# An attention and expert-layer kernel: 36 operations of a computed schedule go back to where the scheduler puts them

## Chip, cores, metric

The kernel runs on one core of a Trainium2 chip. Its time is the device time of one execution in microseconds (us); the profile is the hardware profiler's record of one execution. TensorE (PE) multiplies matrices, VectorE (DVE), ScalarE (ACT) and GpSimd (POOL) do the elementwise work, SyncE (SP) and ScalarE issue the transfers (DMA).

## The reference

Attention over 4 batches, 8 heads, 768 positions and 64 features, in which each query sees its neighbours (less than 16 positions away) and one summary key and value for each block of 32 positions; its output, 3072 tokens of 512 features, goes through a layer with a softmax gate and a layernorm:

```python
k_sum = k.reshape(B, H, nb, block, D).max(axis=3)
v_sum = v.reshape(B, H, nb, block, D).mean(axis=3)
scores_l_m = np.where(mask_l, scale * q @ k.T, -1e9)          # |i - j| < 16
scores_s = scale * einsum('bhsd,bhnd->bhsn', q, k_sum) + log(block)
a = softmax(concat([scores_l_m, scores_s]))
x = (a @ concat([v, v_sum])) as (3072, 512)
h = x @ w_in                                                  # (512, 1024)
solu = h * softmax(h)
ln = (solu - mean) / sqrt(var + 1e-6) * g_ln
return ln @ w_out                                             # (1024, 512)
```

(The lines are shortened to what is computed.)

## The kernel before

The 3072 tokens are worked on in 24 tiles of 128. Every float32 product with weights is made of three: a value is split into a part rounded to the matmul's format (names ending in h: xh, lh, and the first half of w) and the rest (xl, ll), and TensorE adds low·high, high·low and high·high in PSUM, about 0.23 us each. For the first eight tiles `first` (line 949) multiplies each tile with w_in into the banks h; from then on `first_two` (968) takes two tiles at once with seven block products in place of eight, into hu, hf and hl, for which ws_own, ws_v, w1s, w3s (sums of blocks of weights) and sums (sums of blocks of x) are made once on VectorE, GpSimd and ScalarE. `second` (1144) multiplies with w_out into the bank o, from which ScalarE (1150) or VectorE (1152) writes os; a transfer takes os to the output from ScalarE's queue (1154).

The attention of a step goes: scores into the PSUM tiles s_0l, s_0r (695); VectorE adds the mask, gives e and the negative maximum nm (714); ScalarE's exponentials (722) with their sum z; VectorE's 1/z (728); e times 1/z on VectorE or GpSimd (406, 407); transposes on TensorE into t_0l, t_0r (750), copied to at (399, 400); products with the values into x (797); x is split into xh (399) and xl (406, 806). The layer between is: hm, the row maximum of h, and its sign turned (1026, 1028); ScalarE's exponentials he (1031); hz, its inverse (1034, 1037); VectorE's he times h (1039) with the mean nmu (1042); ScalarE's centring (1051) and sq, the sum of squares (1054); GpSimd's tiny operations for y (1057 to 1064); transposes or a pass through memory (lt, tbl) and the split into lh and ll. Weights raw are converted through cv to w by integer operations (490 to 525). kw are keys with their block maxima ksum (562), vt values, to which the transfer of line 658 adds the block means vsum.

The PSUM tiles that end in l and r are two halves of one buffer, each in a bank of its own (`halves=True`); this stays.

The program has no loop on the chip: Python writes out every instruction. Each operation is recorded by `op` in an object of class `Plan`, with a cost for each engine that could do it, and given to the engines by `issue`. `issue` works out a due time for each operation, changes due times by a list of fixed random seeds (`SEARCHED`), and `order` then simulates a list schedule: it gives each operation an engine, a start and a place. In the kernel before, `move` comes after it: for each of 36 entries (number of the operation, engine, number of another operation) it takes the operation out of its line and puts it behind the other in the line of the engine named, using that engine's form of it, and merges the lines again. Each engine runs its own line in order, and waits for the others by semaphores. The zero matmuls of line 1336 are put in by `issue` where TensorE would have waited by the plan, in the first 80 us of it.

Of the kernel before, what the change touches and what calls it, by code (L numbers as in the profile page):

```python
# [63 lines left out]
class Buf:  # L64


    def __init__(self, make, prev=()):
        self.make, self.prev, self.tile = make, prev, None
        self.ops, self.writers, self.readers, self.gone = [], {}, {}, False
# [16 lines left out]
class Plan:  # L86
# [29 lines left out]

    MOVES = ((77, "act", 109), (290, "act", 294), (242, "act", 290), (214, "act", 301), (391, "act", 354),
        (540, "act", 547), (602, "act", 582), (613, "act", 612), (664, "act", 668), (679, "act", 672),
        (1396, "act", 1196), (1875, "act", 1855), (100, "dve", 45), (146, "dve", 130), (203, "dve", 155),
        (322, "dve", 388), (314, "dve", 364), (371, "dve", 314), (452, "dve", 410), (419, "dve", 418),  # L120
        (663, "dve", 560), (706, "dve", 707), (678, "dve", 660), (869, "dve", 812), (1223, "dve", 1222),
        (1287, "dve", 1224), (1864, "dve", 1874), (606, "pool", 1150), (561, "pool", 606), (615, "pool", 585),
        (562, "pool", 615), (589, "pool", 588), (680, "pool", 1154), (814, "pool", 1300), (753, "pool", 1302),
        (909, "pool", 1303),)

    def __init__(self):
        self.ops, self.rings, self.banks, self.idle, self.slots = [], {}, {}, None, []
        self.turns, self.homes, self.last, self.shrunk = {}, {}, {}, set()
# [75 lines left out]
    def issue(self):  # L204

        for o in self.ops:
            o.left = len(o.deps)
            for d in o.deps:
                d.users.append(o)
        sorted_ = [o for o in self.ops if not o.left]  # L210
        for o in sorted_:
            for u in o.users:
                u.left -= 1
                if not u.left:
                    sorted_.append(u)
        for o in reversed(sorted_):
            o.due = min([u.due for u in o.users] + ([o.prio] if "pe" in o.can else []), default=o.prio)
            if "sp" in o.can:
                o.due = o.prio
        for seed in self.SEARCHED:  # L220
            self.shift(seed)
        order = self.move(self.order())
        at, done = self.START, set()
        for o in order:
            if o.engine == "pe":
                while at + self.SYNC < min(o.start + o.late, self.FILL):
                    at += self.keep_up(at, done)
                at = max(at - o.late, o.start) + o.cost * (2 if o.start < self.COLD else 1)
            done.add(o)
            o.fn()  # L230

    def move(self, order):


        moved = {self.ops[o]: (e, self.ops[p]) for o, e, p in self.MOVES}
        key = {o: float(i) for i, o in enumerate(order)}
        lines = {}
        for o in order:
            if o not in moved:
                lines.setdefault(o.engine, []).append(o)  # L240
        todo = list(moved)
        while todo:
            o = next(x for x in todo if moved[x][1] not in todo)
            todo.remove(o)
            e, p = moved[o]
            lines[e].insert(lines[e].index(p) + 1, o)
            key[o] = key[p] + 0.01
            o.engine, (o.cost, o.fn) = e, o.can[e]
            o.start = min(o.start, p.start)
        done, out = set(), []  # L250
        while any(lines.values()):
            heads = [x[0] for x in lines.values() if x and x[0].deps <= done]
            o = min(heads, key=key.get)
            lines[o.engine].pop(0)
            done.add(o)
            out.append(o)
        return out

    def shift(self, seed):

# [1121 lines left out]
```

## Time and profile before

| | |
|---|---|
| median of 3 runs | 360.62 us (360.47 to 361.37) |
| the profiled execution | 360.37 us, of which the span of its instructions 358.6 us |
| granted TensorE clock | 1.00 over the whole span |
| TensorE busy | 353.7 us, 99% of the span |
| VectorE, ScalarE, GpSimd busy | 300.5, 279.9, 159.4 us (84, 78, 44%) |
| the chain that ended last | 88% TensorE, 4% ScalarE, 4% transfers, 2% VectorE |

The span is from the first instruction to the last; the time has 1.77 us more around it. A busy TensorE is at work on some matmul; a hole is time in which it waits. The rows further down give for each instruction its start, its duration and, in brackets, how long its engine stood idle ahead of it and for what.

### The profile page before, as it was taken

To read this page: it belongs to the slowest core of one execution; us is meant where nothing else is said; L and a number is where in the kernel's file an instruction comes from. 1 tells how busy PE (TensorE), PEld (TensorE's weight loads), DVE (VectorE), ACT (ScalarE), POOL (GpSimd) and SP (SyncE) were. 2 spreads that over 40 slices of the span, in tenths; PEclk is the share of its full clock that TensorE was granted. 3 is DMA by queue.
4 is the path that set the end of the run, shared out by engine and by line. 5 is a ranking of instruction groups with operands and counts; after the bars stand their busy time and mean duration, and the time that the engine had idled before them with its cause. 6 is when DMAs were issued, how large, how long until landed. Compare 5 with 4: busy or idle time off the path is not lost.

```text
span 358.6 us, 9381 instructions
## 1 busy us (share of the span) xinstructions
PE 353.7 (99%) x3332; PEld 277.3 (77%) x3332; DVE 300.5 (84%) x962; ACT 279.9 (78%) x814; POOL 159.4 (44%) x293
## 2 busy tenths in 40 slices
PE   8999999999999999999999999999999999999996
PEld 3538767778777887787888888888888888888886
DVE  4989999998999998998699998887897996947331
ACT  4888998998869988799698696895896896946320
POOL 6612430267869899225815247150335054533300
PEclk9999999999999999999999999999999999999999
DMA  7999994144525445448389393475264282344711
GB/s 248 417 412 406 357 409 162 62 115 148 172 69 185 137 149 193 141 158 289 101 275 290 112 277 131 128 255 172 80 208 148 59 287 90 117 149 153 229 58 58
DMA packets 28530, 68.19 MB, mean 190 GB/s; under 512 B 3852, under 2 KB 13324, under 8 KB 26948
## 3 DMA queue, kind: packets, MB, share of 16 engines
q1 hardware_dynamic: 24620, 60.87, 50.6%
q10 hardware_dynamic: 3864, 6.74, 5.3%
q8 instruction: 26, 0.43, 0.5%
q14 instruction: 20, 0.16, 0.1%
HBM read 49.55 MB, written 15.73 MB: 182 GB/s over the span
## 4 chain that ended last, share of the span: by engine, by line
PE 88%; ACT 4%; DMA 4%; DVE 2%; issue 0%; POOL 0%; ACTq 0%
PE o L1144 36%; PE hu L968 13%; PE h L949 10%; PE x L797 6%; PE hl L968 6%; PE hf L968 3%; DMA qt<-in_q 2%; PE s_0l L695 2%; PE s_1l L695 2%; PE t_0l L750 2%; PE t_1l L750 2%; ACT e L722 2%; PE vs_ps L582 1%; PE vs_ps L1336 1%; DMA raw<-in_w_in 1%; PE x L1336 1%
## 5 line engine op out<-in xcount | busy, mean ns | idle before, releaser
L1144 PE MATMUL o<-w,lh 128*128 128x512 f32 (+1 forms) x400 | 128.1, 386 | 0.0
L1144 PEld LDWEIGHTS o<-w,lh 128*128 128x128 f32 x400 | 74.1, 188 | 15.6 <-issue 0.6
L1144 PE MATMUL o<-w,ll 128*128 128x512 f32 (+1 forms) x200 | 76.2, 381 | 0.0
L722 ACT ACTIVATE e<-e,nm 128x120 f32<-128x120 f32 x192 | 73.3, 389 | 0.0
L949 PE MATMUL h<-w,xh 128*128 128x512 f32 x128 | 43.0, 400 | 0.2 <-DVE he L1039 0.2
L1144 PEld LDWEIGHTS o<-w,ll 128*128 128x128 f32 x200 | 37.6, 188 | 6.8
L722 ACT ACTIVATION_READ_ACCUMULATOR e<-e,nm 128x1 f32 x192 | 37.3, 194 | 0.0
L949 PEld LDWEIGHTS h<-w,xh 128*128 128x128 f32 x128 | 24.0, 188 | 7.0 <-ACT at L399 0.8
L1051 ACT ACTIVATE he<-he,nmu 128x512 f32<-128x512 f32 x36 | 24.9, 722 | 4.0 <-DVE nmu L1042 3.6
L407 POOL TENSOR_TENSOR ll<-lt,lh 128x512 fp32r<-128x512 f32 x11 | 16.0, 1466 | 26.1 <-DVE lh L400 19.2
L797 PEld LDWEIGHTS x<-at,vt 120*64 120x64 f32 (+1 forms) x768 | 24.4, 138 | 4.1 <-issue 2.4
L624 POOL TENSOR_TENSOR st_v<-st_v 96x512 f32<-96x512 f32 (+3 forms) x28 | 23.0, 830 | 8.3 <-DMA st_v<-in_vb 7.7
L797 PE MATMUL x<-at,vt 120*64 120x64 f32 (+1 forms) x768 | 26.5, 224 | 0.0
L1074 DVE STREAM_TRANSPOSE tbl<-he 128x1024 f32<-128x1024 f32 x18 | 22.3, 1239 | 4.4 <-ACT he L1051 2.3
L1054 ACT ACTIVATE sq<-he 128x1024 bf16<-128x1024 f32 x24 | 25.4, 1057 | 0.1
L949 PE MATMUL h<-w,xl 128*128 128x512 f32 x64 | 25.1, 393 | 0.0
L1031 ACT ACTIVATE he<-hs,hm 128x512 f32<-128x512 f32 x24 | 17.2, 719 | 9.1 <-DVE hm L1021 9.1
L406 DVE TENSOR_TENSOR e<-e,z 128x960 f32<-128x960 f32 x18 | 22.3, 1238 | 0.1
L1150 ACT ACTIVATE os<-o,y 128x512 f32<-128x512 f32 x19 | 13.1, 687 | 11.7 <-PE o L1144 11.5
L407 POOL TENSOR_TENSOR xl<-sums,xh 128x256 fp32r<-128x256 f32 (+1 forms) x12 | 12.4, 1035 | 19.4 <-ACT xh L399 19.4
L401 POOL COPY kw<-ksum 128x192 f32<-128x192 f32 x21 | 8.5, 406 | 26.8 <-PE s_0r L695 20.7
L406 DVE TENSOR_TENSOR ll<-lt,lh 128x512 fp32r<-128x512 f32 x25 | 19.6, 802 | 0.5 <-ACT lh L399 0.3
(250 smaller groups left out, 972.1 us busy)
## 6 DMA issues: line engine op xcount, KB each, us to landing
vt<-in_v SPq DMA_DIRECT2D x12, 1024.0 KB
farl<-tbl SPq DMA_DIRECT2D x18, 512.0 KB
lt<-farl SPq DMA_DIRECT2D x72, 128.0 KB
kraw<-in_k SPq DMA_DIRECT2D x16, 400.0 KB
out<-os ACTq DMA_DIRECT2D x23, 256.0 KB
qt<-in_q SPq DMA_DIRECT2D x11, 512.0 KB
raw<-in_w_in SPq DMA_DIRECT2D x8, 512.0 KB
raw<-in_w_out SPq DMA_DIRECT2D x8, 512.0 KB
```

The source lines that it names most:

```text
L406: by = {dve: lambda: nc.vector.tensor_tensor(out=to(), in0=a(), in1=b(), op=kind), pool: lambda: nc.gpsimd.tensor_tensor(out=to(), in0=a() ...
L407: pool: lambda: nc.gpsimd.tensor_tensor(out=to(), in0=a(), in1=b(), op=kind)}
L624: op(pool, 0.15 + w * 0.0021, lambda w=w, o=o: nc.gpsimd.tensor_tensor(out=o.ap[:n, :w], in0=x.ap[:n, :w], in1=x.ap[:n, w:2 * w], op=ALU.add),
L722: nc.scalar.activation(out=e.ap[:, n, :], in_=e.ap[:, n, :], func=AF.Exp, bias=nm.ap[:, n:n + 1], scale=-1.0, accum_out=z.ap[:, n:n + 1])
L797: nc.tensor.matmul(xp()[j * D:(j + 1) * D, i, qs], vs.ap[:k, u, cs], at.ap[:k, u % 2, n[j] + u // 2, :], start=not apart, stop=not apart o ...
L949: nc.tensor.matmul(hp.ap, a.ap[:, c, ts], w.ap[:, i], start=(c == 0 and n == 0), stop=(c == NKC - 1 and n == 2))
L968: nc.tensor.matmul(to.ap, operand(y, n)[:, c], w(c).ap(i), start=first and c == 0 and k == 0, stop=c == 1 and k == 2, skip_group_check=True)
L1031: op(act, 0.71, lambda i=i, hp=hp: nc.scalar.activation(out=part(i), in_=hp(), func=AF.Exp, bias=nm.ap, accum_out=zs.ap[:, i:i + 1]), r=[k ...
L1051: (act, 0.57, lambda sl=sl: nc.scalar.activation(out=e.ap[:, sl], in_=e.ap[:, sl], func=AF.Identity, bias=nmu.ap))], port=True)
L1054: op(act, 1.13, lambda: nc.scalar.activation(out=sq.ap, in_=e.ap, func=AF.Square, accum_out=ss.ap), r=[e], w=[sq, ss])
L1074: op(dve, 1.13, lambda: nc.vector.transpose(out=tb.ap.rearrange("p (q c a) -> p q c a", q=4, a=32), in_=of().rearrange("p (c q a) -> p q c ...
L1144: nc.tensor.matmul(o.ap[:, cols], a.ap[:, f, :], w.ap[:, i, cols], start=(f == 0 and n == 0), stop=(f == NFC - 1 and n == 2))
```

## The change

The table `MOVES` and the function `move` go, and `issue` takes the schedule as `order` gives it:

```diff
-    MOVES = ((77, "act", 109), (290, "act", 294), (242, "act", 290), (214, "act", 301), (391, "act", 354),
...
-        order = self.move(self.order())
+        order = self.order()
...
-    def move(self, order):
-
-
-        moved = {self.ops[o]: (e, self.ops[p]) for o, e, p in self.MOVES}
...
```

TensorE's and SyncE's lines stay the same, instruction for instruction. Thirty of the 36 operations change only their place on their engine. Six change the engine: one high part of a weight conversion (cv_494) from VectorE to ScalarE, the last half of the last output (os) from VectorE to ScalarE, a cast of xh (128x256) from ScalarE to VectorE, and a subtraction xl (128x256) and two additions ws_own (128x512) from GpSimd to VectorE. The line numbers of the kernel after are lower by 36 for all that stands below `move`.

At three places the rows of the program show what changes. The first is ScalarE at about 31 us, where the second half of a tile's xh is cast and the transfer of the block means into vt is issued. Before:

```order
L399 CAST w_578<-cv_494 128x512
L501 ACTIVATE cv_549<-raw_109 128x512
L399 CAST xh_0_119<-x_0_1_554 128x512
L658 DMA vt_1_111<-vsum_114 24x4x512
L399 COPY kw_2_0_609<-kraw_0_155 128x8x96
```

And after:

```order
L363 CAST w_578<-cv_521 128x512
L465 ACTIVATE cv_549<-raw_109 128x512
L622 DMA vt_1_111<-vsum_114 24x4x512
L363 CAST xh_0_119<-x_0_1_554 128x512
L363 COPY kw_2_0_609<-kraw_0_155 128x8x96
```

The cast of xh, which VectorE's xl waits for, has gone behind the issue of the transfer.

The second is at 128 to 138 us: GpSimd, whose line held the subtraction xl and the two additions ws_own around the multiplication of e (e_2_0) by z. Before:

```order
L624 TENSOR_TENSOR st_v_0_0_1744<-st_v_0_0_1744 96x256
L407 TENSOR_TENSOR xl_1_2015<-sums_1_2020,xh_1_2007 128x256
L407 TENSOR_TENSOR ws_own<-w_578,ws_own 128x512
L1058 TENSOR_SCALAR ss_2086<-ss_2086 128x1
L407 TENSOR_TENSOR e_2_0_2022<-e_2_0_2022,z_2_0_2052 128x960
L407 TENSOR_TENSOR ws_own<-ws_own,w_578 128x512
L1060 TENSOR_TENSOR y_202<-ss_2086,mhalf 128x1
```

And after, where these three are gone from it:

```order
L588 TENSOR_TENSOR st_v_0_0_1744<-st_v_0_0_1744 96x256
L1022 TENSOR_SCALAR ss_2086<-ss_2086 128x1
L1024 TENSOR_TENSOR y_202<-ss_2086,mhalf 128x1
L371 TENSOR_TENSOR e_2_0_2022<-e_2_0_2022,z_2_0_2052 128x960
L1021 TENSOR_TENSOR ss_2086<-ss_2086,y_202 128x1 x2
```

VectorE has them in the same stretch after the change, between the maxima hm, the tiny hm of line 1028 (992 after), the block maxima ksum and 1/z:

```order
L364 CAST ws_v<-ws_own 128x512
L370 TENSOR_TENSOR xl_1_2015<-sums_1_2020,xh_1_2002 128x256
L370 TENSOR_TENSOR ws_v<-ws_own,ws_v 128x512
L526 TENSOR_REDUCE ksum_1_2088<-kraw_1_1932 128x24
L990 TENSOR_REDUCE hm_2098<-h_0_2057 128x1
L990 TENSOR_REDUCE hm_2098<-h_1_2035 128x1
L692 RECIPROCAL z_2_0_2052<-z_2_0_2052 128x8
L370 TENSOR_TENSOR ws_own<-w_578,ws_own 128x512
L992 TENSOR_TENSOR hm_2114<-hm_2098 128x1
L526 TENSOR_REDUCE ksum_1_2088<-kraw_1_1932 128x24
L370 TENSOR_TENSOR ws_own<-ws_own,w_578 128x512
L998 TENSOR_SCALAR hz_2121<-hz_2121 128x1
```

Three two-input operations came over, and the tiny hm, for which ScalarE's exponentials wait, has one of them ahead of it.

The third is the end of ScalarE's line, where the last two halves of the output leave. Before (both halves were made by VectorE):

```order
L1150 ACTIVATE os_5147<-o_5093,y_4963 128x512
L1154 DMA out<-os_5147 128x512
L1154 DMA out<-os_5180 128x256
L1154 DMA out<-os_5183 128x256
L1378 UNCONDITIONAL_BRANCH
```

And after:

```order
L1114 ACTIVATE os_5147<-o_5093,y_4963 128x512
L1118 DMA out<-os_5147 128x512
L1114 ACTIVATE os_5180<-o_5127,y_5010 128x256
L1118 DMA out<-os_5180 128x256
L1118 DMA out<-os_5183 128x256
L1342 UNCONDITIONAL_BRANCH
```

The half that TensorE finishes last (o_5127) is now made by ScalarE itself, and both issues stand behind it.

## Rows read from the trace of the kernel before

**Rows 1.** The page: busy us, share of the span and instructions of each engine.

```profile
PE 353.7 (99%) x3332; PEld 277.3 (77%) x3332; DVE 300.5 (84%) x962; ACT 279.9 (78%) x814; POOL 159.4 (44%) x293
```

**Rows 2.** Two stretches: start:end and length, busy us (instructions) of each engine, clock, DMA.

```profile
50.00:75.00 25.00, 24.52 (x257) 18.67 (x253) 24.31 (x82) 22.14 (x66) 6.57 (x10) 1.00 0.43 154
110.00:137.00 27.00, 27.00 (x290) 22.04 (x283) 26.12 (x78) 24.17 (x81) 24.30 (x29) 1.00 0.42 144
```

**Rows 3.** The page: the chain that ended last, by engine.

```profile
PE 88%; ACT 4%; DMA 4%; DVE 2%; issue 0%; POOL 0%; ACTq 0%
```

**Rows 4.** Timeline of ScalarE and its queue at 31 us: start, duration, instruction.

```profile
31.19 1.43 ACTq L658 DMA_DIRECT2D vt<-vsum  x1
31.27 0.56 ACT L399 CAST xh<-x 128x512 fp32r<-128x512 f32 x1
```

**Rows 5.** Timeline of VectorE at 33 us.

```profile
32.94 0.68 DVE L806 TENSOR_TENSOR xl<-x,xh 128x512 fp32r<-128x512 f32 x1
```

**Rows 6.** Timeline of TensorE at 33.7 us.

```profile
33.67 0.51 PE L949 MATMUL h<-w,xl 128*128 128x512 f32 x1
```

**Rows 7.** Timeline of VectorE at 42 to 44 us.

```profile
42.21 0.75 DVE L1039 SCALAR_TENSOR_TENSOR he<-h,hz,he 128x512 f32<-128x512 f32 x1
...
44.04 0.68 DVE L1026 TENSOR_REDUCE hm<-h 128x1 f32<-128x512 f32 x1
```

**Rows 8.** Timeline of TensorE at 43.4 us.

```profile
43.43 0.58 PE L949 MATMUL h<-w,xh 128*128 128x512 f32 x1
```

**Rows 9.** Timeline of ScalarE and its queue, 54 to 57 us.

```profile
54.96 0.59 ACT L399 CAST lh<-lt0l 128x512 fp32r<-128x512 f32 x1 [1.34 <-PE lt0r L750]
55.02 0.81 ACTq L658 DMA_DIRECT2D vt<-vsum  x1
55.88 0.72 ACT L523 ACTIVATE w<-cv,g_sb 128x512 fp32r<-128x512 f32 x1 [0.33 <-DVE nm L714]
```

**Rows 10.** Timeline of VectorE at 57 us.

```profile
57.10 0.69 DVE L1122 TENSOR_TENSOR ll<-lt0r,lh 128x512 fp32r<-128x512 f32 x1 [0.44 <-ACT lh L399]
```

**Rows 11.** Timeline of TensorE at 67 us.

```profile
66.95 0.50 PE L949 MATMUL h<-w,xh 128*128 128x512 f32 x1 [0.24 <-DVE he L1039]
```

**Rows 12.** Timeline of ScalarE, 117 to 123 us.

```profile
117.21 0.59 ACT L399 COPY at<-t_0r 120x512 f32<-120x512 f32 x1 [0.21 <-PE t_0r L750]
...
122.27 0.62 ACT L399 COPY at<-t_1l 120x512 f32<-120x512 f32 x1
```

**Rows 13.** Timeline of TensorE at 123 us.

```profile
122.99 0.28 PE L695 MATMUL s_0l<-kw,qt 64*64 64x120 f32 x1
```

**Rows 14.** Timeline of VectorE, 131 to 139 us.

```profile
131.83 1.01 DVE L1028 TENSOR_TENSOR hm<-hm 128x1 f32<-128x1 f32 x1
...
138.08 0.76 DVE L853 TENSOR_TENSOR sums<-x,sums 128x256 f32<-128x256 f32 x2 [1.48 <-ACT xh L399]
138.75 0.68 DVE L406 TENSOR_TENSOR xl<-x,xh 128x512 fp32r<-128x512 f32 x1
```

**Rows 15.** All instructions of line 1028: duration in ns, least/median/most, first and last start.

```profile
L1028 DVE TENSOR_TENSOR hm<-hm x8: 107/169/1012, 39.4 to 131.8; 128x1 f32<-128x1 f32 x8
```

**Rows 16.** Timeline of GpSimd, 130 to 135 us.

```profile
130.83 0.74 POOL L407 TENSOR_TENSOR xl<-sums,xh 128x256 fp32r<-128x256 f32 x1
131.53 1.29 POOL L407 TENSOR_TENSOR ws_own<-w,ws_own 128x512 f32<-128x512 f32 x1
...
133.18 1.79 POOL L407 TENSOR_TENSOR e<-e,z 128x960 f32<-128x960 f32 x1
```

**Rows 17.** Timeline of TensorE at 140 us.

```profile
139.98 0.39 PE L968 MATMUL hf<-w,xl 128*128 128x512 f32 x1
```

**Rows 18.** Timeline of VectorE and of ScalarE's queue at the end, 352 to 358.6 us.

```profile
353.37 0.48 DVE L1152 TENSOR_SCALAR os<-o,y 128x256 f32<-128x256 f32 x1 [7.27 <-PE o L1144]
...
353.88 2.34 ACTq L1154 DMA_DIRECT2D out<-os  x2
...
355.37 0.48 DVE L1152 TENSOR_SCALAR os<-o,y 128x256 f32<-128x256 f32 x1 [1.52 <-PE o L1144]
```

More of the change, by code (lines that the diff above doesn't have):

```diff
@@ L115 @@
         -704973400, 25379729, -590422927, -115574272, -202041329, -486402956,
-    MOVES = ((77, "act", 109), (290, "act", 294), (242, "act", 290), (214, "act", 301), (391, "act", 354),
[L118 to L124, printed above, removed]
     def __init__(self):
@@ L230, in issue @@
             o.fn()
-    def move(self, order):
-        moved = {self.ops[o]: (e, self.ops[p]) for o, e, p in self.MOVES}
[L236 to L257, printed above, removed]
     def shift(self, seed):
```

## The prediction

> **What bounds the kernel now.** I read the page first. TensorE is busy in all but five of 358.6 us [rows 1], and the chain that ended last is 88% TensorE [rows 3]: TensorE is the clock, so a change that leaves its instructions and their order alone can only put holes between them or close holes. The order of the two programs on TensorE and SyncE is the same instruction for instruction, the zero matmuls included. So the prediction is a list of holes. The table by stretches says where there is room for any [rows 2]: in 50 to 75 us TensorE is 24.52 of 25 busy and VectorE 24.31, the one stretch where VectorE and ScalarE feed TensorE just in time (the chain runs there over the two of them); in 110 to 137 us TensorE is full, but VectorE has 26.12 of 27 us of work, ScalarE 24.17 and GpSimd 24.30, so little slack is left for anything late. From 75 us on TensorE runs back to back, and what it loses there it keeps to the end. Only behind its last matmul does another engine end the run.
>
> Thirty of the moved operations stay on their engine and only change place; six also change engine. For each I took from the trace when it ended, who used its result first and how long that user could have waited. Most come out at nothing: their result is used half a microsecond or more after the new end too, and the matmuls that stand in TensorE's queue ahead of the user are the cover. Five places are left.
>
> **Place 1, 31 us: +0.34.** Before, ScalarE rounds xh (31.27) ahead of the issue of the vt transfer, which then occupies its queue from 31.19 to 32.62 [rows 4]: the issue was reached early and waited beside the cast. After, the issue stands first (see the order of ScalarE), and the cast comes behind it, 32.66 to 33.24 in place of 31.84 by the 0.56 of its row plus sequencing. VectorE's xl, which needs it and started 32.94 [rows 5], then starts about 33.28, 0.34 later, and the xl matmul at 33.67 [rows 6] had been waiting for exactly that xl (32.94 + 0.68 = 33.62), so TensorE gets the whole 0.34. Bounds: nothing, if the issue takes less time there (the same line took 0.81 at 55.02 [rows 9], which would end it at 32.0, early enough); 0.34, if it takes its 1.43 again. I take 0.34, since it is the same issue after the same landing.
>
> **Place 2, 44 us: +0.25.** VectorE's hm (0.68, of which about 0.60 shows as step to the next instruction) goes from behind two he operations to ahead of them. The first he ended at 42.96 (42.21 + 0.75) [rows 7], and frees the PSUM bank for the matmul at 43.43 [rows 8], which stands behind six zero matmuls in TensorE's queue: 0.47 of slack less what a semaphore takes. An end at 43.6 makes it start at about 43.68: +0.25, and 0 if the zero matmuls run late too.
>
> **Place 3, 50 to 75 us: −0.44, a gain.** Before, ScalarE holds the lh cast and a DMA issue ahead of w (55.88): it idles 1.34 us for the transposes and another 0.33 [rows 9]. After, w goes first, into that idle time, and the second lh cast can follow the first at about 55.5 (54.96 + 0.59) and not only behind w at 56.5 (55.88 + 0.72, less the overlap): up to 1.0 earlier. VectorE waits for this second lh 0.44 us [rows 10], its one idle time for ScalarE there. A queue that is otherwise full gains what it idled: 0.44, and the matmul at 66.95, which waits 0.24 for VectorE's he [rows 11], and those at 75 us come earlier. Bounds: −1.0, the whole of ScalarE's gain, and 0, if ScalarE gives it back (a 0.84 us copy of kw goes from 73.89 to about 60.5).
>
> **Place 4, 117 to 143 us: +0.77.** Two things add up. (a) The at copy that ran at 117.21, ahead of two exponentials that waited for VectorE's hm, goes behind them [rows 12]: ScalarE loses an idle half microsecond that it had used, and all behind it is 0.5 later. The at copy at 122.27 ended 122.89, and the scores matmul, which takes over its PSUM banks, started 122.99 [rows 13]: 0.10 of slack, so +0.40. (b) Three tensor_tensor operations, 0.74 and twice about 1.29 on GpSimd [rows 16], return to VectorE: two of 0.69 (as VectorE's 128x512 in [rows 10]) and one of half the columns, 0.42 with its fixed part (an estimate from those), 1.80 together. VectorE idles 1.48 us at 138.08 for ScalarE's xh [rows 14], so this alone would be nearly hidden, and it saves something: its tiny hm [128,1] took 1.01 us at 131.83 where the median of eight is 0.17 [rows 14, 15], and it ended at 132.84, GpSimd's ws_own (131.53 + 1.29) at 132.82 [rows 16]. So a two-input operation of VectorE waited for one of GpSimd to its end. That 0.84 goes with ws_own. But then hm stands directly behind ws_own on VectorE, and GpSimd's e multiply (1.79, [rows 16]) is ready as soon as z is done, one place ahead of ws_own: it waits for VectorE's port, gets it next, and hm, or the second ws_own, waits 1.79. The balance on VectorE is 1.80 − 0.84 + 1.79 − 1.48 = 1.27 late at xl, which ended 139.43 (138.75 + 0.68); the hf matmul that reads it ran at 139.98 [rows 17], 0.55 later, of which a semaphore takes some 0.05. So TensorE gets 1.27 − 0.50 = 0.77, and (a)'s 0.40 lies inside it. Bounds: 0 (an earlier hole moves TensorE so that both fit) and 0.40 + 1.79 = 2.19 (the wait falls where nothing is idle). The cast of xh that comes over from ScalarE at 123 us (0.29 on VectorE) is in the noise of these.
>
> The Trainium skill, SBUF — State Buffer, section Who interferes with whom, says that a VectorE instruction with two SBUF inputs contends with a GpSimd instruction that reads SBUF, and that whoever issues second is blocked until the first has finished; issue order decides. By that rule the e multiply blocks hm only if it issues first, else it waits itself: the term would be +0.77 by the first and +0.40 by the second. The row at 131.83 agrees that the loser waits to the end of the other; no row shows who is served first when both wait.
>
> **Place 5, the end: +0.34.** Before, both halves of the last output are written by VectorE, at 353.37 and 355.37, and each is sent off at once; the second issue ends at 356.22 (353.88 + 2.34), and the span 2.38 us later [rows 18]. After, the last half is made by ScalarE, and both issues stand behind it on ScalarE's queue, so the half that was ready at 353.85 leaves last. The os on ScalarE starts when VectorE's did and takes about as long (estimate from [rows 18]: 0.48), so the first issue ends at 356.22, and a second of 0.34 follows: the span ends 0.34 later. Upper bound 0.68 (both transfers also share the way). Nothing lies beside it.
>
> **Sum.** 0.34 + 0.25 − 0.44 + 0.77 + 0.34 = 1.26 us on the profiled execution's 360.37 (a span of 358.6 and 1.77 around it): 361.63. The median of the runs, 360.62, lies 0.25 above the profiled one; with that, 361.9. The bounds: lowest 0 + 0 − 1.0 + 0 + 0.34 = −0.66, 360.0; highest 0.34 + 0.25 + 0 + 2.19 + 0.68 = 3.46, 364.1, and 0.5 more for the seven moves behind 162 us, which I cost at nothing.
>
> **Rivals.** *The port isn't lost* (chance 0.25): VectorE's instructions follow each other without a gap and hm keeps ahead of the e multiply. Then place 4 costs 0.40, the sum is 0.34 + 0.25 − 0.44 + 0.40 + 0.34 = 0.89, the time 361.5. For it: VectorE needs no semaphore from another engine there. Against: hm's 1.01 us [rows 14] is the same meeting, and there VectorE lost. *All hidden but the end* (0.10): zero matmuls and slack take up places 1, 2 and 4, and 3 gains nothing; 0.34 stays: 361.0. The change would in effect do nothing. *Faster* (0.13): place 3 gives the whole 1.0 and TensorE has it at 75 us, while places 1, 2 and 4 are hidden: −0.66, 360.0; below 359.5 it decides only if the stretch 50 to 75 us gains more than 1.4 us, that is, if w, brought forward, also lets the he and xl chain behind it close up. Rows 2 speak against that: VectorE has only 25 − 24.31 = 0.69 us of idle time there, so this is the ceiling for anything that VectorE passes on. *More than the sum* (0.10): the port wait of 1.79 falls where nothing covers it, or one of the moves after 162 us costs too: 363.3 to 364.6.
>
> **How the numbers follow.** Forecast 361.9, with 0.42 for it (361.4 to 362.7). Range 360.2 to 364.2. A measurement of this kernel tells 0.3% from no change, 1.1 us: faster is below 359.5, slower above 361.7. Slower: the larger part of the forecast's case (0.33), the worst one (0.10) and a part of the rival at 361.5 (0.09), 0.52. Faster: the better half of its rival, 0.07. The rest, 0.41, is the same.
>
> **What would show it.** Right: the cast of xh ends after 33.2 and the first xl matmul behind it slips; w runs in the idle time before lt0r's cast and VectorE's 0.44 at 57 us is gone; the scores matmul of 122.99 starts later against the matmuls before it; a VectorE operation of 1 to 2 us of the shape [128,1] or ws_own at 133 to 135 us; the two last issues back to back. Wrong: TensorE shows new idle time elsewhere, above all after 150 us, or as much idle time as before and a span that differs only at the end.

## The result, and the profile after

| | before | after |
|---|---|---|
| median | 360.72 us (6 runs, 360.47 to 361.37) | 362.95 us (6 runs, 362.47 to 363.39) |
| ratio to before | | 1.0060, 95% interval 1.0047 to 1.0072 |
| the profiled execution, and its span | 360.37 us, 358.64 us | 363.39 us, 361.67 us |

The kernel after is slower by 2.23 us, 0.6%. The forecast was 361.9 with a range of 360.2 to 364.2: the direction and the range held, the size was 1.0 us short. Why it was short, and which terms were right only by luck, is the rest of this document.

The page of after answers to [rows 1] and [rows 3]: busy times, and the chain that ended last.

```profile
PE 353.7 (98%) x3332; PEld 277.0 (77%) x3332; DVE 305.6 (84%) x964; ACT 281.2 (78%) x815; POOL 158.7 (44%) x290
...
PE 78%; DVE 12%; ACT 3%; DMA 3%; SPq 1%; issue 1%; ACTq 0%; DVEq 0%
```

TensorE does the same 353.7 us of work in a longer span, so holes were added and no work; VectorE's part of the chain went from 2% to 12%. TensorE's waits (line waited for: us in total, times, longest) name most of them:

```profile
PE vs_ps L1300 <- DVE zero L388: 1.0, 1, 1.0
PE o L1108 <- DVE w L489: 0.9, 1, 0.9
PE s_1l L659 <- DMA qt<-in_q: 0.9, 1, 0.9
PE s_0l L659 <- DMA qt<-in_q: 0.5, 1, 0.5
PE s_1l L659 <- ACT at L363: 0.4, 1, 0.4
PE s_0l L659 <- issue: 0.3, 1, 0.3
```

The first is there before too. The list holds only waits of some length; the 0.24 us at 34 us in the next table is not in it. Since TensorE's instructions are the same and in the same order, the start of one matmul in both timelines says how late TensorE is there, and a place's cost is the step between two such points:

| matmul (line of before) | before | after | late by | step |
|---|---|---|---|---|
| vs_ps (582) | 19.95 | 20.54 | 0.58 | 0.58, loads at the start |
| h (949) | 34.24 | 35.05 | 0.82 | 0.24, place 1 |
| h (949) | 45.48 | 46.52 | 1.03 | 0.21, place 2 |
| h (949) | 66.95 | 67.64 | 0.69 | −0.34, place 3 |
| s_0l (695), behind o | 76.42 | 77.90 | 1.48 | 0.79, place 3, not foreseen |
| s_0l (695) | 122.99 | 124.76 | 1.78 | 0.30, place 4a |
| s_1l (695) | 137.27 | 139.63 | 2.36 | 0.58 |
| s_1r (695) | 137.28 | 140.12 | 2.84 | 0.48 |
| hl, second (968) | 143.43 | 145.99 | 2.56 | −0.28; place 4b with the two above 0.78 |
| end of the execution | 360.37 | 363.39 | 3.02 | 0.46, place 5 |

From 146 us to the last matmul TensorE stays 2.56 to 2.57 late. So this execution is 3.02 us longer, of which 0.58 arises before any moved operation: TensorE waits for the first loads of the queries there. The second profile of after, below, shows that this part is chance, and not the change. (The 0.54 for the end in two of the expectations below was taken from spans rounded to tenths; it is 0.46.)

VectorE's timeline of after at 74 us (start, duration, instruction) and GpSimd's show the step of 0.79, with the matmul of TensorE that waits for it:

```profile
73.99 0.63 DVE L770 TENSOR_TENSOR xl<-x,xh 128x512 fp32r<-128x512 f32 x1
74.55 1.94 DVE L489 SCALAR_TENSOR_TENSOR w<-cv,g_sb,w 128x512 fp32r<-128x512 f32 x1
```

```profile
74.15 1.79 POOL L371 TENSOR_TENSOR e<-e,z 128x960 f32<-128x960 f32 x1
```

```profile
76.54 0.50 PE L1108 MATMUL o<-w,lh 128*128 128x512 f32 x1 [0.89 <-DVE w L489]
```

The weights w take 1.94 us where the eight of this line have a median of 0.75 (only one other is long, 1.23 at 72.73, behind GpSimd's cv). GpSimd's e multiply runs until 75.94, and w ends 0.55 after that. The matmul o that needs this w starts at 76.54. At 135 us it is the same meeting, and the one that the prediction named; VectorE's and GpSimd's timelines of after:

```profile
134.52 0.18 DVE L692 RECIPROCAL z<-z 128x8 f32<-128x8 f32 x1
134.63 0.63 DVE L370 TENSOR_TENSOR ws_own<-w,ws_own 128x512 f32<-128x512 f32 x1
135.19 1.74 DVE L992 TENSOR_TENSOR hm<-hm 128x1 f32<-128x1 f32 x1
```

```profile
134.78 2.13 POOL L371 TENSOR_TENSOR e<-e,z 128x960 f32<-128x960 f32 x1 [0.70 <-DVE z L692]
```

e begins at 134.78, is held up by ws_own (its 1.79 becomes 2.13), and then keeps hm, 128 numbers, until 136.91; hm ends at 136.93. (The texts below call this the port, or the lock: one of the two engines waits until the other's whole operation is done.) The meeting of before, 1.01 us, is in [rows 14 to 16]. ScalarE idles 3.69 us ahead of the exponentials, which wait for hm, and its two at copies come behind them; TensorE's scores wait for these copies:

```profile
136.96 0.69 ACT L995 ACTIVATE he<-h,hm 128x512 f32<-128x512 f32 x1 [3.69 <-DVE hm L992]
...
139.00 0.58 ACT L363 COPY at<-t_0l 120x512 f32<-120x512 f32 x1
139.48 0.59 ACT L363 COPY at<-t_0r 120x512 f32<-120x512 f32 x1
```

```profile
139.63 0.41 PE L659 MATMUL s_1l<-kw,qt 64*64 64x120 f32 x2 [0.40 <-ACT at L363]
140.12 0.31 PE L659 MATMUL s_1r<-kw,qt 64*64 64x120 f32 x1
```

s_1l starts when the first copy has ended (139.58), s_1r when the second has (140.07): these are the steps of 0.58 and 0.48.

At 32 us ScalarE's xh stands behind the issue, as the order says (ScalarE and its queue, answering to [rows 4]):

```profile
31.63 1.45 ACTq L622 DMA_DIRECT2D vt<-vsum  x1
33.12 0.59 ACT L363 CAST xh<-x 128x512 fp32r<-128x512 f32 x1 [1.07 <-PE s_0r L659]
```

and at the end of the span (ScalarE and its queue, answering to [rows 18]) both issues stand behind os:

```profile
357.98 0.47 ACT L1114 ACTIVATE os<-o,y 128x256 f32<-128x256 f32 x1 [5.06 <-PE o L1108]
358.48 0.83 ACTq L1118 DMA_DIRECT2D out<-os  x2
```

0.83 for the two: the second issue, directly behind the first, ends 0.49 after it (0.45 for itself and a gap of 0.04), and not 0.34.

### The profile page after: what moved, and what is told of

Read it like the earlier page. It is cut to its first block, busy times and chain, and to the rows that moved or that the text cites. A ratio compares the mean times of both kernels' runs of the same rounds, so it can differ in the third digit from the quotient of the medians.

```text
span 361.7 us, 9382 instructions
## 1 busy us (share of the span) xinstructions
PE 353.7 (98%) x3332; PEld 277.0 (77%) x3332; DVE 305.6 (84%) x964; ACT 281.2 (78%) x815; POOL 158.7 (44%) x290
## 4 chain that ended last, share of the span: by engine, by line
PE 78%; DVE 12%; ACT 3%; DMA 3%; SPq 1%; issue 1%; ACTq 0%; DVEq 0%
PE o L1108 32%; PE hu L932 12%; PE h L913 8%; PE hl L932 6%; PE x L761 5%; PE hf L932 3%; DMA qt<-in_q 3%; PE s_1l L659 2%; PE s_0l L659 2%; PE t_0l L714 2%; DVE ws_own L370 2%; PE vs_ps L546 1%; PE vs_ps L1300 1%; DVE e L678 1%; PE t_1l L714 1%; DVE ksum L526 1%
## 5 line engine op out<-in xcount | busy, mean ns | idle before, releaser
L1114 ACT ACTIVATE os<-o,y 128x512 f32<-128x512 f32 (+1 forms) x20 | 13.5, 675 | 17.3 <-PE o L1108 17.1
L588 POOL TENSOR_TENSOR st_v<-st_v 96x512 f32<-96x512 f32 (+3 forms) x28 | 22.2, 801 | 8.3 <-DMA st_v<-in_vb 7.8
L1022 POOL TENSOR_SCALAR ss<-ss 128x1 f32<-128x1 f32 x24 | 9.9, 413 | 26.4 <-ACT sq L1018 23.7
L365 POOL COPY kw<-ksum 128x192 f32<-128x192 f32 x21 | 9.3, 444 | 27.5 <-PE s_0r L659 22.1
```

Source lines behind the costliest of these rows:

```text
L588: op(pool, 0.15 + w * 0.0021, lambda w=w, o=o: nc.gpsimd.tensor_tensor(out=o.ap[:n, :w], in0=x.ap[:n, :w], in1=x.ap[:n, w:2 * w], op=ALU.add),
```

## The experiments

All but a_hm and after_again are the kernel before with a few entries of the table taken out, so that only these operations go back (u_midact_nofill has one edit more). The diffs name the entries that go, with the label of the run, and not whole lines of the kernel. The line numbers are those of before, in after_again those of after. Medians are of 5 to 12 runs beside 21 to 29 runs of before on the same chip (360.52, 360.65 and 360.50 in the three groups).

| | median | to before | ratio, 95% interval | late behind 146 us by its trace, less the start |
|---|---|---|---|---|
| u_end: place 5 | 361.19 | +0.67 | 1.0009 to 1.0027 | 0.05, and 0.45 at the end |
| u_midact: 290, 242 | 360.06 | −0.46 | 0.9978 to 0.9995 | −0.68 |
| u_middve: 322, 314, 371 | 361.68 | +1.16 | 1.0021 to 1.0043 | 0.96 |
| u_mid: both, with 214, 391 | 360.98 | +0.46 | 1.0004 to 1.0021 | 0.44 |
| u_port: place 4b | 361.31 | +0.66 | 1.0009 to 1.0028 | 0.65 |
| u_540: place 4a | 361.72 | +1.07 | 1.0022 to 1.0045 | 1.25 |
| u_early: places 1, 2 | 361.19 | +0.54 | 1.0004 to 1.0021 | 0.39 |
| a_hm: after, one move more | 362.48 | +1.83 | 1.0036 to 1.0062 | 1.28 (after: 1.99) |
| u_rest: the moves costed at nothing | 360.66 | +0.16 | 0.9984 to 1.0012 | 0.02 |
| u_540_port: place 4 whole | 361.54 | +1.04 | 1.0006 to 1.0038 | 1.12 |
| u_midact_nofill | 359.11 | −1.39 | 0.9930 to 0.9968 | (another TensorE line) |
| after_again | 362.89 | +2.39 | 1.0032 to 1.0073 | 2.25 |

The last column is worked out as in the table above: the lateness at the last matmuls less that of vs_ps at 20 us, from one execution each.

**The end.**

```diff
-(1875, "act", 1855), (1864, "dve", 1874),
```

> The kernel before with only the two moves at the end (1864, 1875) undone: place 5 alone. By the traces of before and after (from the last matmul on the after kernel is 0.54 us longer) +0.54 us; by the prediction's term +0.34; rival, the end is set by the last transfer's own way and not by its place in the queue: within 0.1 of before. In the profile the two last issues on ScalarE's queue stand back to back and TensorE's starts are those of before.

TensorE is not late anywhere by more than chance, and the span ends 0.45 later after the last matmul. The queue is it: the half that was ready waits for the other, and the two issues take 0.83 together here too. The rival, the transfer's own way as the bound, said less than 0.1 and is out.

**Place 3 in two parts, and whole.**

```diff
-(290, "act", 294), (242, "act", 290),                                  u_midact
-(322, "dve", 388), (314, "dve", 364), (371, "dve", 314),               u_middve
-(214, "act", 301), (391, "act", 354), and the five above               u_mid
```

> The kernel before with only 290 and 242 undone, so that ScalarE does w in its idle time ahead of the lh cast: the gain that the prediction claimed at place 3. By the prediction -0.44 us; by the trace of after, where the h matmul of 66.95 us came 0.31 nearer, -0.31; rival, ScalarE or VectorE gives it back before 75 us: 0. VectorE's wait of 0.44 us at 57 us should be gone in all cases.

> The kernel before with only 322, 314 and 371 undone (VectorE, 70 to 75 us), which the prediction costed at nothing. Theory: the later w of line 525 falls under GpSimd's e multiply and is shut out until it ends, which gave +0.85 us at 75 us in the trace of after: +0.85 here. Rival, that meeting came only because the whole stretch was about 0.7 us late in after: 0, and w takes about 0.7 us in the profile.

> The kernel before with all seven moves of 54 to 75 us undone (290, 242, 214, 391, 322, 314, 371). By the trace of after the two parts add up, -0.31 and +0.85 less 0.07: +0.47 us; by the prediction's term -0.44. If the parts don't add, the stretch is bound by something that neither part alone shows, and the sum lies outside +0.2 to +0.7.

The first part is the gain that the prediction claimed. ScalarE's timeline with 290 and 242 undone, answering to [rows 9]:

```profile
53.95 0.72 ACT L523 ACTIVATE w<-cv,g_sb 128x512 fp32r<-128x512 f32 x1
55.39 0.59 ACT L399 CAST lh<-lt0l 128x512 fp32r<-128x512 f32 x1 [0.72 <-PE lt0r L750]
55.87 0.59 ACT L399 CAST lh<-lt0r 128x512 fp32r<-128x512 f32 x1
```

w runs in what was idle, the second lh starts at 55.87 in place of 56.51, and VectorE's two ll follow each other (56.40 and 57.01) with no wait between them, where [rows 10] has 0.44. The kernel is faster than before, and TensorE is busy without a break from 32 to 75 us in this trace. The second part is the meeting: the rival, that it came only because after was late there, fell. VectorE and GpSimd with 322, 314 and 371 undone, nothing else being late:

```profile
73.53 0.64 DVE L806 TENSOR_TENSOR xl<-x,xh 128x512 fp32r<-128x512 f32 x1
74.09 1.94 DVE L525 SCALAR_TENSOR_TENSOR w<-cv,g_sb,w 128x512 fp32r<-128x512 f32 x1
```

```profile
73.69 1.79 POOL L407 TENSOR_TENSOR e<-e,z 128x960 f32<-128x960 f32 x1
```

In before, w was ahead of e:

```profile
73.58 0.73 DVE L525 SCALAR_TENSOR_TENSOR w<-cv,g_sb,w 128x512 fp32r<-128x512 f32 x1
```

```profile
73.79 0.73 POOL L401 COPY kw<-ksum 128x192 f32<-128x192 f32 x1 [1.55 <-DVE ksum L562]
74.49 1.79 POOL L407 TENSOR_TENSOR e<-e,z 128x960 f32<-128x960 f32 x1
```

Two shifts make the meeting. With the three moves undone xl stands ahead of w, which starts 0.51 later; and VectorE makes the ksum that GpSimd's kw waits for ahead of its first w and not behind it, so that kw (72.88) and, behind kw, e start earlier, e by 0.80. The whole, +0.46, is what the trace of after said (+0.45 for its two steps). The parts sum to +0.70 by the medians and +0.28 by the traces; with intervals of about 0.4 to either side this does not decide whether they add.

**Place 4 in two parts, and whole.**

```diff
-(602, "act", 582), (613, "act", 612), (664, "act", 668), (679, "act", 672), (663, "dve", 560),
-(706, "dve", 707), (678, "dve", 660), (606, "pool", 1150), (561, "pool", 606), (615, "pool", 585),
-(562, "pool", 615), (589, "pool", 588), (680, "pool", 1154),           u_port
-(540, "act", 547),                                                     u_540
 all fourteen                                                           u_540_port
```

> The kernel before with only the thirteen moves of 122 to 145 us undone (three additions and subtractions go back from GpSimd to VectorE, with their neighbours): place 4b alone. Theory of the port: the tiny hm is shut out for about 1.6 us by GpSimd's e multiply, and TensorE loses 0.8 us (0.12 + 0.47 + 0.48 - 0.26 in the trace of after; 0.77 by the prediction). Rival, the lock is lost by the other engine here, where nothing is 1.8 us late: hm takes under 0.3 us and the loss is below 0.3.

> The kernel before with only 540 undone (the at copy on ScalarE at 117 us): place 4a alone. By the prediction +0.40 less the 0.17 that TensorE waits at 142.66 anyway, +0.23; by the trace of after, where the scores matmul of 122.99 came 0.32 later, +0.32 or, less the same 0.17, +0.15; rival, a hidden loss: 0.

> The kernel before with 540 and the thirteen moves of 122 to 145 us undone together: the whole of place 4, as it is in after. Separately they cost 1.07 and 0.66. Theory: 540 alone is dear because a VectorE subtraction (w1s) is then shut out for 2.47 us by two GpSimd operations that the other moves had put there; with those back on VectorE that meeting is gone, and the pair costs 0.30 + 0.79 = 1.1, as in the trace of after, or a little less. Rival, the two are independent: 1.7.

With 4b alone undone hm is shut out as in after: VectorE's row at 133.44, answering to [rows 14]:

```profile
133.44 1.75 DVE L1028 TENSOR_TENSOR hm<-hm 128x1 f32<-128x1 f32 x1
```

and TensorE loses 0.65. The surprise is 540 alone: 1.07 and not 0.2. TensorE's step at 122.99 is 0.31, as in after; then t_0l, at 135, is 0.88 later still. VectorE's w1s of before, and VectorE and GpSimd of that kernel at 130 us:

```profile
129.59 0.68 DVE L406 TENSOR_TENSOR w1s<-ws_own,w1s 128x512 fp32r<-128x512 f32 x1
```

```profile
129.50 1.31 DVE L406 TENSOR_TENSOR ws_v<-ws_own,ws_v 128x512 fp32r<-128x512 f32 x1
130.73 2.47 DVE L406 TENSOR_TENSOR w1s<-ws_own,w1s 128x512 fp32r<-128x512 f32 x1
```

```profile
129.47 0.73 POOL L624 TENSOR_TENSOR st_v<-st_v 96x256 f32<-96x256 f32 x1
130.16 1.25 POOL L407 TENSOR_TENSOR xl<-sums,xh 128x256 fp32r<-128x256 f32 x1
131.37 1.29 POOL L407 TENSOR_TENSOR ws_own<-w,ws_own 128x512 f32<-128x512 f32 x1
```

w1s, 0.68 in before, takes 2.47: it is shut out by xl and, without a chance between them, by ws_own, the two that the other moves had brought to GpSimd. A delay of some tenths on VectorE (ws_v at 129.50, in before at 128.98) was enough to put it behind them. 1/z and GpSimd's e come behind w1s, e at 134.59 and not 133.18, and t_0l transposes e. With all fourteen undone these two are on VectorE, w1s takes 0.70 again, and the pair costs 1.04, not 1.73 (by the traces 1.12, not 1.90): the parts are not independent, as was expected.

That the pair costs more than 4b alone has a cause of the same kind. ws_v takes 0.68 in u_port; in u_540_port and in both profiles of after GpSimd's st_v starts just ahead of it (in after at 131.07, until 131.99) and shuts it out:

```profile
131.32 1.22 DVE L370 TENSOR_TENSOR ws_v<-ws_own,ws_v 128x512 fp32r<-128x512 f32 x1
```

VectorE has no idle time from there to hm, so hm comes 0.54 later by it. Without it the pair would cost 1.12 − 0.54, about 0.6, as much as 4b alone; this is an estimate from these rows, and no run took it apart.

**hm ahead of 1/z, in after.** The table and `move` are kept, with one entry:

```diff
-    MOVES = ((77, "act", 109), ...
+    MOVES = ((643, "dve", 642),)
```

> The kernel after with one move: the tiny hm (643) of 135 us goes ahead of 1/z, so that it is done when GpSimd's e multiply, which waits for z, can begin. Nothing else changes place. If the loss of place 4b is the lock, hm takes 0.2 us in place of 1.74, ScalarE's exponentials start some 2 us earlier and the time falls by 0.5 to 0.9 from 362.95, to about 362.2. Rival, the loss is the 1.8 us of work that came back to VectorE: 362.8 to 363.0.

VectorE's timeline:

```profile
134.17 0.16 DVE L1028 TENSOR_TENSOR hm<-hm 128x1 f32<-128x1 f32 x1
134.24 0.20 DVE L728 RECIPROCAL z<-z 128x8 f32<-128x8 f32 x1
134.36 0.64 DVE L406 TENSOR_TENSOR ws_own<-w,ws_own 128x512 f32<-128x512 f32 x1
134.91 0.95 DVE L562 TENSOR_REDUCE ksum<-kraw 128x24 f32<-128x768 f32 x1
135.78 1.42 DVE L406 TENSOR_TENSOR ws_own<-ws_own,w 128x512 f32<-128x512 f32 x1
```

hm takes 0.16, and ScalarE begins the exponentials at 134.36, where after had 136.96. Now the second ws_own is shut out (1.42); ScalarE's w3s waits for it, TensorE does not. TensorE's steps of 0.58 and 0.48 at s_1l and s_1r are gone; behind 146 us it is 1.14 to 1.28 late and not 1.99. The median, +1.83 to before, lies below the 2.23 and 2.39 of the two groups of after by 0.4 to 0.6, at the lower edge of what was expected; the intervals of the ratios overlap, so the times alone would not carry it, but the trace does. The 1.8 us of work that came back to VectorE are still there, and most of the loss is gone: the lock was the cost. Two smaller things went the same way in this trace: ws_v took 0.68, and the first ws_own (0.64) stands behind hm. They are not what decides, since u_port has ws_v at 0.68 and ws_own ahead of hm, and with hm at 1.75 still loses 0.65.

**Places 1 and 2, and the rest.**

```diff
-(77, "act", 109), (203, "dve", 155), (100, "dve", 45), (146, "dve", 130),                  u_early
-(452, "dve", 410), (419, "dve", 418), (814, "pool", 1300), (753, "pool", 1302),
-(909, "pool", 1303), (869, "dve", 812), (1223, "dve", 1222), (1287, "dve", 1224),
-(1396, "act", 1196),                                                                       u_rest
```

> The kernel before with only 77, 203, 100 and 146 undone: places 1 and 2. By the prediction 0.34 + 0.25 = +0.59 at 47 us; by the trace of after 0.23 + 0.26 - 0.09 = +0.40; rival, VectorE and ScalarE bound the stretch from 49 to 75 us and take it up there: below 0.2 in the time though TensorE is late at 47 us.

> The kernel before with the nine moves undone that the prediction and the trace of after both cost at nothing (452, 419 at 90 us; 814, 753, 869, 909, 1223, 1287, 1396 behind 162 us): within 0.2 us of before. Rival, a meeting of VectorE and GpSimd that comes only in before's timing, as in the kernel with 540 undone: over 0.4 us slower, with a new wait of TensorE behind 85 us.

0.17 and 0.22 by the trace at 34 and 45 us, all of it kept to the end: the rival, that the stretch behind takes it up, fell. At place 2 the first he ends at 43.97 (43.23 + 0.74), and the matmul behind the six zero matmuls starts at 44.03, as the prediction had it. The rest is nothing, as costed.

**After once more.** 

> The kernel after once more, for a second profile: in its first profile the first matmuls waited 0.58 us longer for the loads of the queries than in before, with no moved operation ahead of them. If that is chance of the execution, the waits at 10 and 14 us differ here again while the steps from 31 us on repeat (0.24, 0.2, -0.34, +0.79, +0.30, +0.79 and 0.54 at the end, 2.5 in all); if it belongs to the change, it is 0.5 to 0.6 again. Median 362.7 to 363.1.

Its TensorE waits have no load among them:

```profile
PE vs_ps L1300 <- DVE zero L388: 1.0, 1, 1.0
PE o L1108 <- DVE w L489: 0.9, 1, 0.9
PE s_1l L659 <- ACT at L363: 0.4, 1, 0.4
PE s_0l L659 <- issue: 0.3, 1, 0.3
PE h L913 <- DVE xl L770: 0.2, 1, 0.2
```

vs_ps starts at 19.81, 0.14 earlier than in before, and the steps that follow repeat (0.40, 0.21, −0.35, 0.77, 0.38, 0.82, and 0.45 at the end). So the 0.58 of the first profile is chance of the execution; over the fourteen profiles vs_ps starts between 19.81 and 20.54, though no moved operation stands ahead of it.

**Beyond both kernels.** u_midact is faster than before. Its TensorE is without a wait between 32 and 75 us, but part of its work there are zero matmuls, some of which stand where their successor could have started; so, on top of it:

```diff
-    COLD, FILL = 6.9, 80.0
+    COLD, FILL = 6.9, 25.0
```

> The best kernel so far (before without 290 and 242, 0.46 us faster than before), with no zero matmuls behind 25 us of the plan: eighteen fewer, about 0.22 us each. In before the matmul behind three of them at 25.84 could have started 1.37 us earlier and the one behind six at 42.31 0.47 earlier, so TensorE may gain 0.4 to 0.9 up to 48 us; the stretch 50 to 75 us then has to follow. Expected 0.3 to 0.7 faster than without this edit, about 359.5; rival, the stretch 50 to 75 us is bound by VectorE from its own work and gives it back: 360.0; second rival, the granted clock falls while TensorE waits: slower than before.

359.11, 1.39 below before, where u_midact was 0.46 below: 0.93 more, which is more than was expected. Stretches of u_midact and of this kernel (columns as in [rows 2]):

```profile
50.00:75.00 25.00, 25.00 (x261) 18.84 (x254) 24.82 (x82) 22.70 (x67) 7.79 (x10) 1.00 0.46 162
```

```profile
32.00:50.00 18.00, 17.39 (x168) 11.88 (x160) 17.76 (x68) 16.98 (x55) 5.61 (x6) 1.00 1.03 382
50.00:75.00 25.00, 23.81 (x252) 18.66 (x248) 24.95 (x83) 22.75 (x67) 7.59 (x10) 1.00 0.45 163
```

TensorE idles 1.19 us there and VectorE 0.05: VectorE is now the bound of the stretch, and the zero matmuls had taken the place of real ones. The granted clock stayed at 1.00 in both stretches. How the gain divides between 26, 42 and 64 us was not taken apart.

## Why the prediction held, and where it was short

- **What bounds.** Right: TensorE's line is the clock and keeps every hole behind 146 us to the end (2.56 to 2.57 in the first profile of after). "From 75 us on" was too early: at hl, 143 us, it made up 0.28, since it had waited there in before.
- **Place 1, +0.34.** 0.24, 0.40 and 0.42 in the three traces with after's order, 0.17 in u_early. The mechanism is shown: xh stands behind an issue of 1.44 to 1.45 us in all four, as assumed. Why this issue is so long and the one at 55 us takes 0.81 was not tested; SyncE issues three transfers in the same stretch at 31 us and none at 55. The size goes with the start of the issue, which is 31.00 in u_early and 31.05, 31.22 and 31.24 in the three, each less the lateness of vs_ps.
- **Place 2, +0.25.** 0.21 in both profiles of after, 0.22 in u_early, by the path that was named.
- **Place 3, −0.44.** The gain is real: −0.34 at 66.95, and −0.46 in the time of u_midact. But the sentence that most moves "come out at nothing" failed for 322, 314 and 371, three VectorE operations that the prediction does not name. They put w behind the start of GpSimd's e multiply, and the wait of 1.2 us is worth 0.77 to 0.90 by the traces and 1.16 in the time of u_middve. I had the rule, and a row for it at 131.83, and did not ask at the other places what GpSimd does while a moved two-input operation of VectorE runs. This is the miss: with it the sum would have been 1.26 + 0.79 = 2.05. What is left to 2.44 are sizes: 0.31 at place 4, 0.12 at place 5, and −0.04 at the first three together.
- **Place 4, +0.77.** The order in which the two engines are served, which the prediction had chosen without a row, is as chosen: GpSimd first, hm 1.74. The cost, 0.30 + 0.78 = 1.08, is larger by 0.31, because (a) does not lie inside (b): ws_v is shut out by st_v as well, and by the estimate above its 0.54 takes up the slack that (a)'s later start of TensorE would have given. That (b) itself comes to 0.78 where 0.77 was worked out is luck, since the path was another. In after, hm's delay reached TensorE at s_1l and s_1r over ScalarE's two at copies (0.47 of the 0.58, and 0.48); at hf, where I had put it, behind VectorE's xl, nothing was left to pay.
- **Place 5, +0.34.** 0.44 to 0.46 in the four traces that have it, and 0.67 ± 0.3 in the time of u_end: the second issue ends 0.49 after the first and not 0.34.
- **The sum.** By the trace of after 0.24 + 0.21 − 0.34 + 0.79 + 1.08 + 0.46 = 2.44, against 2.23 and 2.39 in the times; 1.26 was predicted. Group by group, undone alone in before, the traces give 0.39 + 0.44 + 1.12 + 0.50 + 0.02 = 2.47 (u_early, u_mid, u_540_port, u_end, u_rest); the medians of these groups add up to 2.87, each known to about 0.3 to 0.6. That the time lies in the range is in part luck too: its upper end came from a 2.19 at place 4 that did not come, and it covered a place that was not on the list.
- **The rivals.** "The port isn't lost" fell at 135 us (hm 1.74 to 1.75 in after, after_again, u_port and u_540_port). "Faster" needed place 3's first part without its second; that is u_midact, and it is faster. "More than the sum" is what came in kind, if not in place: a lock where nothing covered it, at 75 us; the time it gave, 363.3 to 364.6, was not reached.
- What I said would show it came: xh behind the issue, w in the idle time, the later scores, a VectorE operation of 1.74 of the shape [128,1] at 135 us, the two issues back to back. But what I had named as a sign of being wrong came too: TensorE has a new wait of 0.9 at 75 us, where no place was listed.

## What to carry to other kernels

When an operation moves between engines or in its line, ask for each VectorE operation near it that reads two tensors from SBUF (the on-chip memory beside PSUM) what GpSimd runs at that moment: a shift of some tenths can turn into a wait of a whole GpSimd operation, and such waits need not add up from move to move (1.07 and 0.66 apart, 1.04 together). A list of hand-made moves should be undone in groups after it is made: two of these 36 cost 0.46 us. And what stands last on the queue that sends the output is worth its place to the tenth.

## What the hardware showed that was not expected

- When a VectorE two-input operation ended and both GpSimd and VectorE's next were waiting, GpSimd went first in after and u_port (hm 1.74 and 1.75), and in u_540 two GpSimd operations in a row kept VectorE out over both (w1s 2.47 in place of 0.68), although w1s starts in the trace ahead of the second (130.73 and 131.37). GpSimd does not always come first: in before VectorE's ll, shut out by GpSimd's e until 296.77, ends at 297.32, and it is GpSimd's next that is long, 1.74 where ws_own of the same size takes 1.29 in [rows 16]:

```profile
295.67 1.65 DVE L406 TENSOR_TENSOR ll<-lt,lh 128x512 fp32r<-128x512 f32 x1
```

```profile
296.73 1.74 POOL L407 TENSOR_TENSOR ll<-lt,lh 128x512 fp32r<-128x512 f32 x1
```

- That the one that is shut out waits to the end of the other (hm ends at 136.93, e at 136.91) agrees with the Trainium skill, SBUF — State Buffer, section Who interferes with whom, by which the one that issues second is blocked until the first has finished. It also holds for scalar_tensor_tensor (w, 1.94 in place of 0.73). An operation with one input in PSUM was not shut out: xl at 73.99 in after, whose x lies in PSUM, takes 0.63 beside e, and e its usual 1.79.
- Of two transfers issued back to back from ScalarE's queue the first took 0.34 us to issue, the second 0.45 and a gap of 0.04.
- The first loads let vs_ps start anywhere between 19.81 and 20.54 us in fourteen executions, 0.2% of the time.
